# Dummy matmuls ahead of the first scores, two kinds of load on another queue, and 1.5 instead of 1.2 conversion steps a unit, in a fused decay-attention and MLP kernel

## The chip, the core and the metric

The kernel runs on one core of a Trainium2 chip. The metric is device microseconds of one execution; the time of a kernel is the median of its runs. The page of the profile shows one further execution, recorded by the hardware profiler.

## The reference

Attention with a decay, eight batches of eight heads, 576 positions, 64 channels, followed by an MLP with a squared relu on all 4608 tokens:

```python
scores = scale * np.matmul(q, k.transpose(0, 1, 3, 2))
log_f = np.log(np.clip(f, 0.0001, 1.0))
cum = np.cumsum(log_f, axis=-1)
decay = cum[:, :, :, None] - cum[:, :, None, :]
scores = np.where(causal, -1000000000.0, scores + decay)
scores = scores - np.max(scores, axis=-1, keepdims=True)
attn = np.exp(scores)
attn = attn / (np.sum(attn, axis=-1, keepdims=True) + 1e-09)
x = np.matmul(attn, v)            # then (batch, seq, heads * channels)
h = np.maximum(x @ w_in, 0.0)     # 512 -> 2048
out = h * h @ w_out               # 2048 -> 512
```

The MLP's weights arrive as float64 and are read as pairs of 32-bit words.

## The kernel before

**Slots.** The 64 heads (NH) are taken one after the other, and each head is NU = 6 units of scores; a slot is one unit. The loop at the end of the kernel runs over slots n from -12; the first score is in slot 0. In each slot the program emits the unit's score matmuls and its exponential, the product with V of the unit two slots back (LAG), parts of the division by the denominator (`finish`), the events entered for this slot with `at` (loads, maxima), then conversion steps (`cv`) and, from slot 60, halves of MLP steps (`fill`). Each slot has two halves. The program order of TensorE (PE), ACT, DVE and POOL is this order of tracing, kept by `in_order`. SP only issues DMAs and keeps the order too.

**Heads 0 to 13** (`h < NWHOLE`) use fp32 operands. `load_whole` brings q and k of a head into one of two buffers (`rl` in the profile, L251), two heads ahead, and `load_rounded` brings the same q and k rounded to fp32r through POOL's queue (`rk`, L244). `load_cum` (L236 and L238) adds the rows of the cumulated decay. In the head before, `max_units` computes the row maxima from the rounded copy: six matmuls (L302), each with a reduction on DVE (`tcol`, L308) in two PSUM banks, and five small stores of a column of maxima into a row of the whole q (L314, from SP). A score matmul (L335, masked blocks L337) has q, k, the decay and that row as its 67 rows, so it waits for the store. The exponential is L351 on ACT, the product with V L398, `v` is loaded at L258. `finish` moves denominators through DRAM (L423, L428, L431) and multiplies at L434.

**Weights.** `weight_ops` is a generator. `stage` loads one of 32 blocks of 512 KB (L164), up to four blocks ahead of the conversion; five steps convert a block from float64 words to a pair of fp32r parts: four operations on DVE (L184, L189, L194, L196), an absolute value and a copy on ACT (L173, L201), a subtraction on POOL (L202). `convert(n)` takes n steps. RATES gives the steps a slot: slots before -6, slots -6 to -1, slots 0 to 47, and later ones.

**MLP.** Token chunks of 256: `mlp1` has 12 matmuls (L464) and `mlp2` 6 (L487) for each of 16 blocks of the hidden layer. They start at slot 60, on the block pairs that are converted by then, are paced over the remaining slots of a batch, and go on alone after the last head.

**PSUM.** Bank 7 is unused until the first MLP chunk takes it as `o1`. `mz` is a bf16 tile of 128x448, zero but for its last 128 columns (a causal mask).

**Semaphores.** In the compiled program the DMAs of SP carry eight semaphores in turn, and an issue waits until the eighth DMA before it has landed.

Of the kernel before, what the change touches and what calls it, by code (L numbers as in the profile page):

```python
# [9 lines left out]
F32 = mybir.dt.float32  # L10
F32R = mybir.dt.float32r
I32 = mybir.dt.int32
# [21 lines left out]
def decay_attention_relu2_kernel(  # L34
# [18 lines left out]
    nc = tc.nc  # L53

    NH, D, _, S = qk.shape
    P = 2 * D
# [21 lines left out]
    psum = ctx.enter_context(tc.tile_pool(name="psum", bufs=1, space=bass.MemoryType.PSUM))  # L78
# [3 lines left out]
    def bank(use):  # L82
# [7 lines left out]
    MW = 448  # L90
    mz = cpool.tile([P, MW], BF16, name="mz")
    nc.gpsimd.memset(mz, 0.0)
    nc.gpsimd.affine_select(
        out=mz[:, MW - P:], in_=mz[:, MW - P:], pattern=[[-1, P]],
# [6 lines left out]
        out=eye, in_=eye, pattern=[[-1, P]],  # L101
# [23 lines left out]
    def load_f():  # L125
        nc.sync.dma_start(out=fr[:NH, 0, :], in_=f)
# [29 lines left out]
    def weight_ops():  # L156

        staged, mags = {}, {}

        def stage():  # L160
            i = len(staged)
            if i < NW:
                raw = staged[i] = wk.tile([P, 2 * DM], I32, name=f"w{i}", bufs=1)
                nc.sync.dma_start(out=raw, in_=(w_in, w_out)[i % 2][i // 2].bitcast(I32))  # L164

        def words(i):
            w = staged[i].rearrange("p (n t) -> p n t", t=2)
            return w[:, :, 0], w[:, :, 1]

        def magnitude(i):  # L170
            if i < NW:
                mags[i] = wk.tile([P, DM], F32, name="wmag", bufs=1)
                nc.scalar.activation(out=mags[i], in_=words(i)[1].bitcast(F32), func=AF.Abs)  # L173

        stage()
        stage()
        yield
        magnitude(0)
        yield
        for i in range(NW):  # L180
            low, high = words(i)
            mag = mags.pop(i)

            nc.vector.tensor_scalar(mag, mag, MAG_LOW, MAG_HIGH, ALU.max, ALU.min)  # L184
            yield
            w = wk.tile([P, DM], F32, name="osb")
            wi = w.bitcast(I32)

            nc.vector.tensor_scalar(  # L189
                wi, mag.bitcast(I32), 3, 0x3FFFFFFF, ALU.logical_shift_left, ALU.bitwise_and,  # L190
            )
            magnitude(i + 1)
            yield
            nc.vector.scalar_tensor_tensor(wi, high, -0x40000000, wi, ALU.bitwise_and, ALU.bitwise_or)  # L194
            yield
            nc.vector.scalar_tensor_tensor(wi, low, 29, wi, ALU.logical_shift_right, ALU.bitwise_or)  # L196
            while len(staged) < min(i + 1 + DEPTH, NW):
                stage()
            yield
            hl = wk.tile([P, 2, DM], F32R, name=f"w{i}", bufs=1)  # L200
            nc.scalar.copy(out=hl[:, 0], in_=w)  # L201
            nc.gpsimd.tensor_tensor(out=hl[:, 1], in0=w, in1=hl[:, 0].bitcast(F32), op=ALU.subtract)  # L202
            split_w.append(hl)
            yield
# [17 lines left out]
    NU = len(UNITS)  # L222
# [9 lines left out]
    def load_cum(h, k):  # L232

        if h == 0:
            for i, c in enumerate(cum):
                nc.sync.dma_start(out=f32(k[D + i:D + i + 1, :]), in_=c[h:h + 1])  # L236
        else:
            nc.sync.dma_start(out=f32(k[D:D + 2, :]), in_=cum_dr[h])  # L238

    def load_rounded(h):  # L240

        x = rounded[h % 2]
        state[h] = dict(r2=x[:, 0], kl0=x[:, 1], p={})
        nc.gpsimd.dma_start(out=x[:D], in_=qk[h])  # L244
        if cum:
            load_cum(h, x[:, 1])

    def load_whole(h):

        x = state[h]["whole"] = whole[h % 2]  # L250
        nc.sync.dma_start(out=x[:D], in_=qk[h])  # L251
        if cum:
            load_cum(h, x[:, 1])

# [278 lines left out]

    RATES = (1, 2, 1.2, 2.5)
    LAG = 2
    NA = H * NU

# [2 lines left out]
    MAXIMA = (0, 0.5, 1, 1.5, 2, 2.5), (1.5, 2, 2.5, 3, 3.5, 4)  # L542
# [48 lines left out]
    def cv(k):  # L591
        owed[0] += k
        convert(int(owed[0]))
        owed[0] -= int(owed[0])
# [3 lines left out]
    def at(n, half, do, *args):  # L598
        events.setdefault((n, half), []).append(lambda: do(*args))
# [6 lines left out]
    for h in range(NH):  # L606
        split = h >= NWHOLE
        if split:
            at((h - 2) * NU + LOAD, 0, load, h)
            for part in range(4):  # L610
                at((h - 1) * NU + SPLIT[part], 1, prep, h, part)
        else:
            if h > 1:
                at((h - 3) * NU + 3, 0, load_rounded, h)
                at((h - 2) * NU + 5, 1, load_whole, h)
        at((h - 1) * NU + VLOAD, 1, load_v, h)
        at((h - 1) * NU + VSPLIT, 1, split_v, h)
        for i, x in enumerate(MAXIMA[split]):
            at((h - 1) * NU + int(x), int(2 * x) % 2, max_unit, h, i)
    for b in range(B):  # L620
        at(ready[b] - 2, 0, split_x, b * S // T, b + 1)
    load_f()
    load_rounded(0)
    convert(1)
    load_whole(0)
    decay()
    load_cum(0, rounded[0][:, 1])
    load_cum(0, whole[0][:, 1])
    store_cum()
    load_rounded(1)  # L630
    load_whole(1)
    for n in range(-2 * NU, last_slot + 1):
        live = 0 <= n < len(slots)
        split_last()
        if live:
            h, u = slots[n]
# [11 lines left out]
        for do in events.get((n, 0), ()):  # L648
            do()
        wr = RATES[0 if n < -NU else 1 if n < 0 else 2 if n < NA else 3]  # L650
        cv(wr / 2)
# [49 lines left out]
```

## Time and profile before

| | us |
|---|---|
| median of three runs | 1267.6 |
| the three runs | 1256.87, 1269.65, 1267.6 |
| span of the profiled execution, its own time on the page | 1272.5 |
| PE busy | 1225.8 |
| DVE busy | 780.7 |
| ACT busy | 703.2 |
| POOL busy | 368.3 |

The profiled execution is 2.9 us above the slowest of the three runs; the page gives no time outside its span. A row of the timeline has start, duration, engine, line, operation, output<-input, shape, count, and in brackets how long the engine sat idle before it and what ended that. A row of the table of windows has, for a stretch of the span, the busy time of each engine with its instructions, the granted TensorE clock (1.00 is full), the share of the DMA engines and the GB/s. SPq is SP's queue of DMA issues.

### The profile page before, as it was taken

The numbers are of one execution on the slowest core, as the hardware profiler recorded it, in microseconds if no ns is written. First come the engines' busy times: TensorE is split into PE (matmuls) and PEld (weight loads), VectorE is DVE, ScalarE is ACT, GpSimd is POOL, SyncE is SP. The second block draws the span as 40 slices with busy tenths as digits, with TensorE's granted clock in tenths as the row PEclk, the third lists the DMA queues.
The fourth block names the chain that finished last, engine by engine and source line by source line (L and its number), as shares of the span: only waits on it lengthen the run. The fifth ranks groups of instructions, "written<-read, shape, count | busy, mean of one in ns | idle before, by whom it ended". The sixth has DMA issues, their size and how long they took to land.

```text
span 1272.5 us, 23177 instructions
## 1 busy us (share of the span) xinstructions
PE 1225.8 (96%) x7652; PEld 1064.1 (84%) x7652; DVE 780.7 (61%) x2042; ACT 703.2 (55%) x1720; POOL 368.3 (29%) x508
## 2 busy tenths in 40 slices
PE   3997899999999999999999999999999999999998
PEld 2664578788999889999899989998998989999997
DVE  6354887666676667665665576667666767533322
ACT  3453455456666666665656566666666666632332
POOL 3122323333333433332232233333333433200000
PEclk9997699999999999999999999999999999999999
DMA  8566661102121112111111111212121211100000
GB/s 198 117 148 140 158 165 31 52 20 56 40 57 40 52 40 56 38 43 46 33 37 44 35 38 40 57 40 56 40 57 38 53 40 47 26 27 1 17 18 17
DMA packets 115639, 71.90 MB, mean 57 GB/s; under 512 B 97384, under 2 KB 97384, under 8 KB 115520
## 3 DMA queue, kind: packets, MB, share of 16 engines
q1 hardware_dynamic: 114400, 66.30, 21.5%
q0 software_dynamic: 1120, 4.13, 1.5%
q8 instruction: 61, 1.00, 0.3%
q14 instruction: 58, 0.48, 0.1%
HBM read 60.20 MB, written 9.88 MB: 55 GB/s over the span
## 4 chain that ended last, share of the span: by engine, by line
PE 63%; ACT 2%; issue 1%; POOL 1%; DVE 0%; DMA 0%; SPq 0%; POOLq 0%; DVEq 0%
PE bank L464 25%; PE bank L487 24%; PE bank L377 3%; PE bank L344 2%; PE bank L379 2%; PE bank L378 2%; PE bank L302 2%; PE bank L341 2%; ACT ph L366 0%; ACT den L413 0%; ACT r L472 0%; DMA den<-rdr 0%; ACT p L351 0%; POOL v L289 0%; POOL p L353 0%
## 5 line engine op out<-in xcount | busy, mean ns | idle before, releaser
L487 PE MATMUL bank<-w,gh 128*128 128x512 f32 x1152 | 413.6, 400 | 0.0
L464 PE MATMUL bank<-xh,w 128*128 128x256 f32 x2304 | 331.1, 286 | 2.9 <-DVE tcol L308 2.9
L367 DVE TENSOR_TENSOR pl<-p,ph 128x320 fp32r<-128x320 f32 (+4 forms) x300 | 186.2, 621 | 210.3 <-ACT ph L366 200.8
L464 PEld LDWEIGHTS bank<-xh,w 128*128 128x128 f32 x2304 | 301.7, 190 | 12.4 <-DVE tcol L308 3.5
L487 PEld LDWEIGHTS bank<-w,gh 128*128 128x128 f32 x1152 | 217.4, 189 | 39.0
L487 PE MATMUL bank<-w,gl 128*128 128x512 f32 x576 | 226.9, 394 | 0.2 <-DVE gl L475 0.2
L472 ACT ACTIVATE r<-bank 128x256 f32<-128x256 f32 x288 | 110.6, 384 | 209.2 <-PE bank L464 196.6
L473 DVE TENSOR_TENSOR g<-r 128x256 f32<-128x256 f32 x288 | 129.0, 448 | 143.5 <-ACT r L472 142.8
L353 POOL TENSOR_SCALAR_AFFINE_SELECT p<-p 128x128 f32<-128x128 f32 (+1 forms) x250 | 81.0, 324 | 450.5 <-ACT p L351 292.8
L366 ACT CAST ph<-p 128x320 fp32r<-128x320 f32 (+4 forms) x300 | 124.4, 415 | 149.0 <-POOL p L353 147.3
L464 PE MATMUL bank<-xl,w 128*128 128x256 f32 x1152 | 185.3, 283 | 0.0
L308 DVE CUSTOM_DVE_ANT_0 bank<-bank,mz 128x256 f32<-128x256 f32 (+4 forms) x320 | 133.8, 432 | 68.4 <-PE bank L302 67.1
L464 PEld LDWEIGHTS bank<-xl,w 128*128 128x128 f32 x1152 | 158.8, 191 | 0.0
L351 ACT ACTIVATE p<-bank 128x320 f32<-128x320 f32 (+4 forms) x300 | 116.0, 387 | 70.6 <-PE bank L344 66.6
L475 DVE TENSOR_TENSOR gl<-g,gh 128x256 fp32r<-128x256 f32 x288 | 126.3, 438 | 35.4 <-DVE g L473 0.9
L302 PE MATMUL bank<-rk 66*128 66x320 f32 (+4 forms) x384 | 119.0, 340 | 21.5 <-DMA rk<-qkraw 14.3
L474 ACT ACTIVATE gh<-r 128x256 fp32r<-128x256 f32 x288 | 120.5, 418 | 9.1
L487 PEld LDWEIGHTS bank<-w,gl 128*128 128x128 f32 x576 | 109.2, 190 | 14.3 <-DVE gl L475 0.9
L302 PEld LDWEIGHTS bank<-rk 66*128 66x128 f32 (+1 forms) x384 | 73.3, 198 | 40.3 <-issue 18.6
L377 PE MATMUL bank<-pl,vh 128*65 128x320 f32 (+4 forms) x350 | 99.4, 284 | 1.7 <-ACT den L413 1.5
L378 PE MATMUL bank<-ph,v 128*64 128x320 f32 (+4 forms) x350 | 94.8, 271 | 0.0
L379 PE MATMUL bank<-ph,vh 128*65 128x320 f32 (+4 forms) x350 | 93.0, 272 | 0.0
(66 smaller groups left out, 1531.6 us busy)
## 6 DMA issues: line engine op xcount, KB each, us to landing
qkraw<-in_qk SPq DMA_DIRECT2D x50, 288.0 KB
v<-in_v SPq DMA_DIRECT2D x64, 160.0 KB
den<-rdr SPq DMA_DIRECT2D x64, 144.0 KB
out<-osb SPq DMA_DIRECT2D x36, 256.0 KB
w<-in_w_in SPq DMA_DIRECT2D x16, 512.0 KB
w<-in_w_out SPq DMA_DIRECT2D x16, 512.0 KB
rl<-in_qk SPq DMA_DIRECT2D x14, 288.0 KB
rk<-in_qk POOLq DMA_DIRECT2D x14, 288.0 KB, 5.2
```

The lines of the kernel that those rows point to most:

```text
L302: nc.tensor.matmul(ps[:m, :n], st["r2"][:D + 2, q0:q0 + m], st["kl0"][:D + 2, k0:k0 + n], start=True, stop=True,)
L308: nc.vector.tensor_tensor_reduce(out=ps[:m, :n], in0=ps[:m, :n], in1=mz[:m, mo:mo + n], op0=ALU.add, op1=ALU.min, scale=-1.0, scalar=init, ...
L366: nc.scalar.copy(out=ph[:kn, :n], in_=p[:kn, :n])
L367: nc.vector.tensor_tensor(out=pl[:kn, :n], in0=p[:kn, :n], in1=ph[:kn, :n].bitcast(F32), op=ALU.subtract,)
L377: nc.tensor.matmul(acc[:D + 1, o], vh, pl[:kn, i], start=first, stop=False)
L378: nc.tensor.matmul(acc[:D, o], vl, ph[:kn, i], start=False, stop=False)
L379: nc.tensor.matmul(acc[:D + 1, o], vh, ph[:kn, i], start=False, stop=last)
L464: nc.tensor.matmul(ph[:, :T], w[:, s, cc], x[:, cc, :], start=(cc == 0 and k == 0), stop=(cc == NCC - 1 and k == 2),)
L473: nc.vector.tensor_tensor(out=g, in0=r, in1=r, op=ALU.mult)
L474: nc.scalar.activation(out=gh, in_=r, func=AF.Square)
L475: nc.vector.tensor_tensor(out=gl, in0=g, in1=gh.bitcast(F32), op=ALU.subtract)
L487: nc.tensor.matmul(po, g[:, ts], w[:, s], start=(fc == 0 and k == 0), stop=(fc == NF - 1 and k == 2),)
```

## The change

Four edits. (1) 24 matmuls are put at the very start of PE's program; two more follow each of head 0's first five maxima and 14 the last one: 48 in all. Each is `mz[:, :128]` (zeros) times `mz`, bf16, 128x128 by 128x448, into bank 7, whose content is used by nobody. (2) The weight blocks are loaded from ACT's queue. (3) The whole q and k of heads 2 to 13 are loaded from ACT's queue; heads 0 and 1 stay on SP's. (4) In slots 0 to 47 a slot has 1.5 conversion steps and not 1.2.

```diff
-                nc.sync.dma_start(out=raw, in_=(w_in, w_out)[i % 2][i // 2].bitcast(I32))
+                nc.scalar.dma_start(out=raw, in_=(w_in, w_out)[i % 2][i // 2].bitcast(I32))
...
-        nc.sync.dma_start(out=x[:D], in_=qk[h])
+        (nc.scalar if h > 1 else nc.sync).dma_start(out=x[:D], in_=qk[h])
...
-    RATES = (1, 2, 1.2, 2.5)
+    RATES = (1, 2, 1.5, 2.5)
...
+    spun = psum.tile([P, 512], F32, name="bank7")
+
+    def spin(n):
+
+        for _ in range(n):
+            nc.tensor.matmul(spun[:, :MW], mz[:, :P], mz, start=True, stop=True)
+
+    for i in range(5):
+        at(int(MAXIMA[False][i]) - NU, int(2 * MAXIMA[False][i]) % 2, spin, 2)
+    at(int(MAXIMA[False][5]) - NU, int(2 * MAXIMA[False][5]) % 2, spin, 14)
+    spin(24)
     load_f()
     load_rounded(0)
     convert(1)
```

## The prediction

> **What bounds the kernel now.** First the slices of the span on the page.
>
> ```profile
> PE   3997899999999999999999999999999999999998
> ...
> PEclk9997699999999999999999999999999999999999
> DMA  8566661102121112111111111212121211100000
> ```
>
> PE is busy nearly all the time, so a microsecond that PE gains early arrives at the end unless a later wait takes it back. Only the first seven slices have holes, and two have a reduced clock; the change works there. Next, windows cut at the heads' first score matmuls: heads 1 to 3, 5, 7, 9, 10 and 11.
>
> ```profile
> 34.39:47.88 13.49, 13.49 (x38) 8.18 (x37) 5.00 (x17) 5.45 (x14) 2.56 (x4) 1.00 0.55 130
> 47.88:61.38 13.50, 13.50 (x39) 8.18 (x38) 6.75 (x20) 5.75 (x14) 2.63 (x4) 1.00 0.42 103
> 61.38:74.87 13.49, 13.49 (x38) 8.18 (x38) 6.69 (x17) 5.00 (x13) 3.28 (x4) 1.00 0.68 154
> ...
> 86.68:98.41 11.73, 7.79 (x40) 4.82 (x38) 6.31 (x18) 6.49 (x15) 2.90 (x4) 1.00 0.93 192
> ...
> 108.90:122.73 13.83, 7.47 (x39) 4.76 (x38) 6.92 (x18) 5.83 (x15) 4.60 (x5) 0.86 0.84 183
> ...
> 134.49:148.42 13.93, 12.08 (x39) 6.63 (x37) 12.00 (x28) 7.83 (x17) 6.60 (x7) 0.68 1.02 235
> 148.42:174.20 25.78, 22.88 (x117) 18.02 (x116) 19.06 (x39) 10.19 (x24) 5.49 (x6) 0.78 0.57 136
> 174.20:195.16 20.96, 20.12 (x118) 16.06 (x117) 16.59 (x36) 11.69 (x28) 5.45 (x5) 1.00 0.61 176
> ```
>
> Heads 1 to 3 take 13.5 us each, with PE busy throughout and a clock shown as 1.00. That 1.00 is not to be believed: here is one form of score matmul in head 2 and in head 5, from the timeline of PE.
>
> ```profile
> 50.66 1.27 PE L335 MATMUL bank<-rl 67*128 67x320 f32 x2
> 51.72 0.31 PE L337 MATMUL bank<-p,mz 128*128 128x128 bf16 x1
> ...
> 88.14 0.70 PE L335 MATMUL bank<-rl 67*128 67x320 f32 x2
> ```
>
> The same work takes 1.27 and 0.70 us. So until about 84.8 us PE ran at half clock, and the view has no record of it. With the clock up, PE is done with head 5 after some 7.8 us (its busy time in the window from 86.68) and then idles. Windows cut where durations change show the clock after that; under them, PE's waits between 14 and 240 us.
>
> ```profile
> 84.78:98.43 13.65, 9.71 (x49) 5.89 (x47) 6.74 (x19) 7.12 (x16) 4.46 (x5) 1.00 0.94 192
> ...
> 118.91:132.56 13.65, 9.83 (x28) 6.38 (x29) 6.60 (x18) 4.67 (x10) 2.29 (x2) 0.50 0.44 88
> ...
> 139.39:159.87 20.48, 17.08 (x50) 10.79 (x51) 14.97 (x30) 8.25 (x19) 7.07 (x7) 0.50 0.71 169
> ...
> PE bank L302 <- DMA rk<-qkraw: 14.3, 1, 14.3
> PE bank L335 <- issue: 5.7, 1, 5.7
> ...
> PE bank L335 <- DMA rl<-tcol: 3.8, 1, 3.8
> ```
>
> At full clock PE outruns the loads, waits 3.8 or 5.7 us at the end of heads 5 and 7 for a store of maxima, and the clock halves; then the slow head hides the next stores, and the clock rises again. All edges lie multiples of 3.41 us apart: 4 of them from 84.78 to 98.43, 6 from 98.43 to 118.91, and so on. What raises the clock I estimate from the matmuls of one stretch:
>
> ```profile
> 23.34:159.87 136.53, 121.48 (x391) 75.32 (x392) 77.64 (x209) 60.04 (x138) 36.72 (x43) 0.85 0.62 140
> ```
>
> For each 3.41 us piece of it I added every matmul's streaming time, weighted by its active rows over 128: 66 or 67 for maxima and scores, 128 for L337, L398 and L464. Streaming times are scaled from the gapless fp32 score of 320 columns, 1.06 us at half clock (50.66 to 51.72), and a quarter of that per column for fp32r and bf16. The clock rose after pieces with a share of 0.756 to 0.77, never after 0.755 or less; it fell after 0.35 or less and stayed after 0.466 or more. Attention alone gives 0.5 to 0.77, so whether it rises depends on how the pieces happen to fall on a head.
>
> **The change part by part.** *Dummy matmuls.* The nearest row in streaming is the MLP's first group at half clock, 12 matmuls of 256 columns in 2.73 us (up to the next L302); `mz` is ready at 1.65.
>
> ```profile
> 1.36 0.29 POOL L93 TENSOR_SCALAR_AFFINE_SELECT mz<-mz 128x128 bf16<-128x128 bf16 x1
> ...
> 14.31 0.82 PE L302 MATMUL bank<-rk 66*128 66x256 f32 x2 [14.31 <-DMA rk<-qkraw]
> ...
> 18.26 0.31 PE L302 MATMUL bank<-rk 66*64 66x64 f32 x1 [0.48 <-DVE tcol L308]
> ...
> 23.16 1.41 PE L335 MATMUL bank<-rl 67*128 67x320 f32 x2 [4.59 <-DMA w<-in_w_out]
> ...
> 154.04 2.08 PE L464 MATMUL bank<-xh,w 128*128 128x256 f32 x8 [2.90 <-DVE tcol L308]
> ...
> 156.77 0.47 PE L302 MATMUL bank<-rk 66*128 66x320 f32 x1
> ```
>
> That is 0.23 us for 256 columns, so 0.40 for 448, and 0.20 at full clock. The first 24 take 4.8 to 9.6 us, end by 11.3 and lie beside the wait to 14.31; a clock that they raise is lost again in the rest of that wait. The other 24 use all 128 rows, with few gaps from the first maximum on, a share near 1: a piece that begins after 14.3 raises the clock by about 21 us, before the first score. Their price: ten of them, 4.0 us at half clock, stand between maxima that DVE spaces anyway (3.95 us from first to last), and 14 need 2.8 to 5.6 us in a wait of 4.6. The first score is late by between 0 and 2 us; I take +1. No row shows that zeros count like data; that is a rival.
>
> [...]
>
> *Heads 0 to 3*, 51.71 us (23.16 to 74.87), would then run as heads 4 to 7 do, 47.86 us (74.87 to 122.73) or 11.97 each, with the clock going up and down. *Moved loads.* The queues at the end of head 5:
>
> ```profile
> 90.33 0.58 SPq L164 DMA_DIRECT2D w<-in_w_in  x1
> ...
> 91.00 1.12 SPq L431 DMA_DIRECT2D den<-rdr  x2
> ...
> 92.21 1.83 SPq L314 DMA_DIRECT2D rl<-tcol  x3
> ...
> 92.33 0.56 POOL L244 DMA_DIRECT2D rk<-in_qk  x1
> ...
> 94.13 0.60 SPq L258 DMA_DIRECT2D v<-in_v  x1
> ...
> 94.83 0.90 SPq L314 DMA_DIRECT2D rl<-tcol  x1
> ...
> 98.38 0.48 PEld L335 LDWEIGHTS bank<-rl 67*128 67x128 f32 x2 [3.90 <-DMA rl<-tcol]
> ```
>
> SP loses 1.44 weight issues a head (7.2 steps, five a block) and one of `rl`, 2.44 by 0.58 = 1.4 us, of which I count half as standing ahead of the stores: -0.7 a head. The same bytes still come. With the DMA engines at 0.94 the last store needs 2.6 us from the end of its issue to the score, and POOL's load, on a queue of its own, shares those engines, so another queue need not let a store overtake. Bounds: 0 to -3.8 a head, the whole wait. *Rate 1.5* adds 0.36 block, 0.19 MB, a head; at head 9's 235 GB/s that is 0.8 us where DMA decides and nothing where it does not: +0.2. So 11.5 a head: -5.8 for heads 0 to 3, -2.0 for heads 4 to 7.
>
> On ACT the 32 + 12 issues cost what they cost SP: 2.8 a head by 0.58, 1.6 us. ACT was busy 5.4 us in heads 1 to 3 (mean), at most 6.8 if all of it grew with the rate: 8.4 of 11.5. Behind a waiting issue stand exponentials, and PE's product with V waits for those; two units of lag cover them. I cost this at 0; without the cover it is rival C.
>
> *Start.* Three weight loads no longer stand ahead of the two rows of cumulated decay in SP's queue:
>
> ```profile
> 0.81 0.58 SPq L126 DMA_DIRECT2D xt<-in_f  x1
> ...
> 3.59 0.64 DVE L132 TENSOR_SCALAR xt<-xt 64x576 f32<-64x576 f32 x1 [0.76 <-DMA xt<-in_f]
> ...
> 6.85 1.31 SPq L236 DMA_DIRECT2D rk<-qkraw  x2
> ```
>
> These issues end at 8.16; f, alone on the engines, was used 2.2 after its issue, so 10.4 instead of 14.3 is the best: 0 to -3.9, and I take half, -2. *Heads 8 and 9* keep their 2.5 steps and their DMA load (1.02 in head 9): -1, of 0 to -4. *Head 10* took 25.78 against 20.96 for the next, with the clock down until 159.87: half the difference, -2.4. *Conversion* ends at slot 76 instead of 82 (91.0 instead of 76.6 of 162 steps are done by slot 48); there PE has three short waits for DVE, 3.3 us in all up to 320 us: -1, of 0 to -3.
>
> ```profile
> PE bank L302 <- DVE tcol L308: 3.3, 3, 1.4
> ```
>
> Sum: +1 -5.8 -2.0 -2 -1 -2.4 -1 = -13.2, on the profiled execution's own 1272.5: 1259.3. That execution lies 4.9 above the median. How long the first stretch stays at half clock depends on where the pieces fall, so I take half of the -5.8 as a gain that the median has already: -10.3 from 1267.6, **1257**.
>
> **Rivals.** *A, the clock holds.* For it: a share of 0.466 is enough to keep the clock. Then a head costs PE 7.9 us and DMA 8.2 (the mean of heads 1 to 3, 1.74 MB, plus 0.19, at 235 GB/s); with 1 us of waiting for a store, 9.2. Heads 0 to 7 go from 99.6 to 73.6, -26; with -1 at the start, -4, -4.8 and -1: -36.8, and with the 2.9 given back, 1234. Against it: both heads that ended at full clock without MLP work beside them waited 3.8 and 5.7. *B, it does not do what it says*: zeros don't raise the clock, or the next pieces lose it at once, and stores stay behind loads. The 14 dummies cost 1.5, and +1.5 -2 -2 -1 -1 gives 1263. The rows from 92.33 to 98.38 speak for its second half. [...] *C, slower.* ACT's in-order queue carries 44 issues, 25.5 us at SP's price, and each waits for the eighth DMA before it, as SP once did for 2.0 us:
>
> ```profile
> SPq L164 <- DMA w<-in_w_out: 2.0, 1, 2.0
> ```
>
> I estimate 1 us for every fourth weight block, 8. If all of it reaches PE: 1257 + 33.5 = 1290. It decides once ACT's waits pass 3.1 us a head (11.5 less 8.4). Against it: the waits are rare on SP, and ACT has that slack.
>
> **How the numbers follow.** Chances: the forecast 0.54, A 0.15, B 0.24, C 0.07. The forecast's own bounds, from the terms above, reach some 12 us down and 8 up; B lies inside. The range takes those in, reaches a little into A's side, and leaves out most of A and all of C: 1242 to 1269. One per cent, about what can be told from no change in this kernel, is 1254.9 to 1280.3. Faster takes A, nearly half of the forecast and a little of B: 0.42; slower is C, 0.07; the rest is 0.51.
>
> **What would show it.** Right: scores of 320 columns at 0.70 us in head 0; heads of 10 to 12 us with gaps at their ends, and half clock after the gaps; first maxima before 14 us; no L164 in SP's queue. Wrong: 1.27 us still in heads 1 to 3 (B); heads near 9 us without gaps (A); exponentials that start late behind ACT's DMA issues while DVE and DMA have time (C).

## The result and the profile after

The change makes the kernel a little slower. The median is 1271.5 us (20 runs, 1261.9 to 1280.4) against 1263.3 us for the kernel before (20 runs, 1256.8 to 1275.6); the ratio is 1.0065, with a 95% interval of 1.0037 to 1.0094. The forecast was 1257, with a range of 1242 to 1269. The profiled execution took 1266.0 us (span 1264.3), 5.5 below its own median; the profile of before, with a span of 1272.5, lay some 11 us above a typical span of its kernel (1263.3 less the 1.7 us that lie around the span here). Read side by side, these two profiles therefore show a gain that the medians don't have.

First the slices of the span and the two hardware queues of the changed kernel's page (packets, MB, share of the DMA engines).

```profile
PE   5987899999999999999999999999999999999998
PEclk8777699999999999999999999999999999999999
...
q1 hardware_dynamic: 108832, 45.98, 15.8%
q10 hardware_dynamic: 5568, 20.32, 5.5%
```

The move was made: 20.32 MB, 32 weight blocks and 12 heads' q and k, now go through ACT's queue (q10). The holes in PE's first slices and the reduced clock beside them are no fewer than before. The start, in the timeline of the changed kernel (SP's issues, one ACT issue, one DVE operation, PE):

```profile
0.81 0.57 SPq L126 DMA_DIRECT2D xt<-in_f  x1
1.44 0.57 SPq L251 DMA_DIRECT2D rl<-in_qk  x1
2.06 2.58 SPq L258 DMA_DIRECT2D v<-in_v  x3
9.27 1.33 SPq L236 DMA_DIRECT2D rk<-qkraw  x2
...
20.70 0.50 SPq L229 DMA_DIRECT2D qkraw<-in_qk  x1
21.29 1.84 SPq L314 DMA_DIRECT2D rl<-tcol  x3
...
0.82 0.38 ACTq L164 DMA_DIRECT2D w<-in_w_in  x1
...
6.20 0.45 DVE L132 TENSOR_SCALAR xt<-xt 64x576 f32<-64x576 f32 x1 [3.37 <-DMA xt<-in_f]
...
17.34 0.55 PE L302 MATMUL bank<-rk 66*128 66x256 f32 x1 [8.92 <-DMA rk<-qkraw]
...
22.69 2.92 PE L627 MATMUL bank<-mz 128*128 128x448 bf16 x14
28.91 0.78 PE L335 MATMUL bank<-rl 67*128 67x320 f32 x2 [3.30 <-DMA rl<-tcol]
29.84 1.27 PE L335 MATMUL bank<-rl 67*128 67x320 f32 x2
```

f was used at 3.59 us before and is used at 6.20 now: a weight block goes out at the same moment on the other queue, and three loads of v follow f on SP's own (e4 below splits the two). The rows of cumulated decay are computed from f, and their issue starts at 9.27 instead of 6.85. The decay is also stored, in two parts, which are out of SP's queue by 10.70 in before. Now the second part goes out at 14.17, as its issue waits until a load of v has landed, the DMA that had carried its semaphore before (SP's waits up to 26 us: us in total, times, longest):

```profile
SPq L146 <- DMA v<-in_v: 1.1, 1, 1.1
```

The load of the stored decay follows at 19.94 instead of 15.04, and behind it the stores of maxima begin at 21.29 instead of 16.69. The first maxima come at 17.34 instead of 14.31, and the first score at 28.91 instead of 23.16. This corrects a sentence of the part on the kernel: SP does not keep the order of the code. `in_order` names only PE, ACT, DVE and POOL; SP's issues are placed by the framework's scheduler, which filled SP's freed time with v and with q and k of head 14 (20.70).

Windows of the changed kernel (start:end and length, busy time of PE, its weight loads, DVE, ACT, POOL, then granted clock, DMA share, GB/s): the last zeros, the wait behind them, the stretch after the clock was lost, heads 0 to 3, 4 to 7, 8 and 9, 10, and the rest.

```profile
22.90:25.60 2.70, 2.70 (x14) 1.18 (x12) 2.56 (x6) 0.99 (x2) 1.80 (x3) 1.00 0.68 150
25.60:28.91 3.31, 0.01 (x1) 0.03 (x1) 1.59 (x4) 0.58 (x2) 0.00 (x0) 1.00 0.39 98
...
29.73:46.80 17.07, 17.07 (x50) 10.67 (x48) 9.85 (x30) 7.50 (x17) 3.80 (x6) 0.50 0.49 133
...
28.91:70.80 41.89, 39.32 (x142) 24.72 (x142) 26.57 (x79) 21.17 (x50) 11.37 (x16) 0.71 0.61 154
70.80:118.75 47.95, 36.91 (x151) 22.15 (x149) 31.38 (x82) 23.88 (x57) 16.08 (x19) 0.82 0.72 168
118.75:144.12 25.37, 23.39 (x74) 14.14 (x74) 20.18 (x45) 13.26 (x29) 10.16 (x11) 0.63 0.65 177
144.12:170.56 26.44, 22.69 (x117) 17.87 (x117) 20.22 (x43) 11.52 (x27) 6.60 (x6) 0.77 0.42 109
170.56:1264.30 1093.74, 1084.38 (x7169) 973.95 (x7167) 667.16 (x1762) 626.19 (x1549) 315.93 (x436) 1.00 0.17 40
```

The same stretches of before (head 10 took 25.78):

```profile
23.16:74.87 51.71, 51.71 (x142) 31.45 (x143) 25.66 (x73) 20.43 (x48) 11.54 (x15) 1.00 0.61 135
74.87:122.73 47.86, 37.56 (x150) 23.87 (x149) 24.19 (x76) 22.38 (x53) 13.07 (x16) 0.89 0.64 139
122.73:148.42 25.69, 23.84 (x74) 14.06 (x74) 20.46 (x47) 13.71 (x30) 9.73 (x11) 0.63 0.67 159
...
174.20:1272.50 1098.30, 1086.75 (x7169) 975.13 (x7167) 676.53 (x1775) 628.78 (x1556) 319.25 (x439) 1.00 0.17 42
```

The zeros did raise the clock (1.00 from 22.90), but PE then idles 3.31 us for the stores of maxima and the clock halves at 29.73, 0.82 us after the first score. What the zeros were to buy is gone before it is used. Between the two profiles: +5.7 to the first score, -9.8 in heads 0 to 3, +0.1, -0.3 and +0.7 in the next groups, -4.6 from head 11 on.

### The profile page after: what moved, and what is told of

Same layout as the page of the kernel before. It is cut to its first block, busy times and chain, and to the rows that moved or that the text cites. A ratio compares the mean times of both kernels' runs of the same rounds, so it can differ in the third digit from the quotient of the medians.

```text
span 1264.3 us, 23245 instructions
## 1 busy us (share of the span) xinstructions
PE 1221.7 (97%) x7700; PEld 1059.9 (84%) x7700; DVE 781.3 (62%) x2042; ACT 703.8 (56%) x1720; POOL 369.2 (29%) x508
## 3 DMA queue, kind: packets, MB, share of 16 engines
q10 hardware_dynamic: 5568, 20.32, 5.5%
## 5 line engine op out<-in xcount | busy, mean ns | idle before, releaser
L475 DVE TENSOR_TENSOR gl<-g,gh 128x256 fp32r<-128x256 f32 x288 | 129.2, 449 | 35.8 <-DVE g L473 0.5
```

The costliest lines, as they stand in the source:

```text
L475: nc.vector.tensor_tensor(out=gl, in0=g, in1=gh.bitcast(F32), op=ALU.subtract)
```

## The experiments

All ratios are to the kernel before, run beside it on the same chip; a ratio is not the quotient of the two medians and differs from it by up to 0.3%. The theory at the outset: the moved loads cost by a later start, and the zeros' clock is lost in the next wait. The rivals: ACT's queue costs in every head, or the zeros or the rate cost.

**The three parts alone**

```
e1: + the 48 matmuls of zeros            e3: RATES = (1, 2, 1.5, 2.5)
e2: stage(): nc.scalar.dma_start(...)    load_whole: (nc.scalar if h > 1 else nc.sync).dma_start(...)
e4: the whole change, and in_order(..., ("PE", "Activation", "DVE", "Pool", "SP"))
```

> The kernel before with the 48 dummy matmuls alone. Theory H (SP's reordered start made the change slower): the dummies are harmless or help; SP's order is that of before, the first score is at 23 to 24.5 us, scores of 320 columns run at 0.70 us in head 0, and the time is 0 to 6 us under before. Theory S (ACT's issues) says the same of this run. Theory D (the dummies themselves cost): 3 to 8 us over before, with a late first score.

> The kernel before with the two kinds of load on ACT's queue alone. Theory H: SP's scheduler, no longer held by the weight blocks, issues three loads of v ahead of the cumulated rows, and the load of q and k of head 14 ahead of the first stores of maxima; first maxima at 17 us, first score at 27 to 29 us, and the time 4 to 10 us over before. Theory S (ACT's in-order issues delay exponentials): also slower by 4 to 10 us, but spread over heads 0 to 9, each 0.5 to 1 us longer, with the first score not later than 25. Theory D: within 2 us of before.

> The kernel before with 1.5 conversion steps a unit alone. Theory H: within 3 us of before, first score at 23.2. Theory R (the extra weight blocks compete for the DMA engines in the first heads): 3 to 8 us over before, heads 4 to 9 longer by 0.5 to 1 us each.

> The changed kernel whole, with SP's issues held in the order of tracing as the other engines' are. Theory H: first maxima at 12 to 14 us, first score at 19 to 24, and the time 5 to 12 us under the changed kernel, so 0 to 5 under before. Theory S: the first score moves, but the time stays within 3 us of the changed kernel's, 6 to 9 over before. Theory R: likewise 3 to 8 over before.

Measured: zeros 1269.2 us, ratio 1.0033 (0.9999 to 1.0066); moved loads 1275.4, 1.0097 (1.0058 to 1.0135); rate 1261.6, 0.9987 (0.9952 to 1.0023); SP in the order of the code 1273.0, 1.0079 (1.0046 to 1.0111). The moved loads are the cost, the rate is nothing that can be told, the zeros gain nothing: their time is the one that theory D named, without the late first score that it went with. PE's timeline with the zeros alone, and the windows up to the clock's fall and from there to its next rise:

```profile
22.29 0.78 PE L335 MATMUL bank<-rl 67*128 67x320 f32 x2
...
23.18 0.70 PE L335 MATMUL bank<-rl 67*128 67x320 f32 x2
...
22.29:25.90 3.61, 2.84 (x12) 1.72 (x12) 3.33 (x10) 2.01 (x5) 1.31 (x2) 1.00 0.99 237
25.90:43.00 17.10, 16.98 (x49) 10.33 (x48) 9.38 (x29) 6.71 (x16) 3.87 (x5) 0.50 0.50 121
```

Here the zeros do all that was hoped: the first score is not late and runs at 0.70 us. The clock is lost 3.61 us later all the same, in attention that kept PE busy for 2.84 of them, and rises again at 43.0. SP in the order of the code did bring the first maxima forward, yet not the time (DVE's first use of f, SP's wait, then PE):

```profile
5.24 0.54 DVE L132 TENSOR_SCALAR xt<-xt 64x576 f32<-64x576 f32 x1 [2.41 <-DMA xt<-in_f]
...
17.75 0.32 SPq L238 DMA_DIRECT2D rk<-cum_dr  x1
...
11.34 0.36 PE L302 MATMUL bank<-rk 66*128 66x256 f32 x1 [2.31 <-DMA rk<-qkraw]
25.45 1.41 PE L335 MATMUL bank<-rl 67*128 67x320 f32 x2 [6.82 <-DMA rl<-tcol]
```

SP now stands until 17.75 for the stored decay, and the stores of the maxima computed from 11.34 on stand behind it. Here no v goes ahead, and f is used at 5.24: of the 2.6 us by which it is late in the whole change, 1.65 come without the loads of v and 1.0 with them.

**The start, one queue each, and before again**

```
e5: the whole change, but stage(): (nc.scalar if i > 5 else nc.sync).dma_start(...)
e6: the kernel before, stage() alone on nc.scalar
e7: SP's first 20 issues in a written order, all but two weight blocks after the first maxima's stores; RATES = (0, 2, 1.5, 2.5)
e8: the kernel before, unchanged
e9: the kernel before, load_whole alone on nc.scalar for h > 1
```

> The whole change, but with the first six weight blocks left on SP's queue, so that SP issues its first loads in the order of before. Theory S (the cost of the moved loads is the later start: f shares the engines with weights, SP issues v first, first score 28.91 instead of 23.16): f lands before 4.0 us, first maxima at 14 to 15, first score 22 to 24, and the time falls from 1271.5 to about 1264 (ratio to before 0.997 to 1.003). Rival T (the cost lies in the later heads, by stores that wait beside loads of another queue or by ACT's issues): first score early, but 1269 or more (ratio 1.004 and up).

> The kernel before with the weight blocks alone on ACT's queue; the q and k loads stay on SP. Theory S: f lands near 6 us and the first score comes at 28 to 29 as with both moves, time 1270 to 1276 (ratio 1.005 to 1.010). Rival U (the q and k loads on ACT, which wait there behind exponentials, are the costly part): first score may be late, but the time is within 3 us of before (ratio under 1.003).

> The kernel before with SP's first twenty issues in an order written out: f, one weight block, the rows of cumulated decay, their store, the second block, head 1's rows, the first maxima's stores, and only then the other blocks; no conversion steps before slot -9, 1.5 a unit later. Theory S (the order of the first loads decides): first maxima at 10 to 12 us, first score at 17 to 20, time 1258 to 1261 (ratio 0.994 to 0.998). Rival V (an early start is given back, since the weight blocks then arrive later and the first heads wait for stores and v, as when all of SP's order was pinned): first score before 21, but head 4 starts no earlier than 70 us at a like clock, and the time is 1263 or more.

> The kernel before once more, for a second profile. Theory W (the half clock up to 84.8 us was one execution's luck): the clock is up before 60 us, heads 0 to 3 take at most 47 us together instead of 51.7, and the span is 1268 or less. Rival X (the kernel before always sleeps that long): scores of 320 columns at 1.27 us up to head 3 or 4, heads 0 to 3 in 50 us or more, span 1270 to 1275.

> The kernel before with only the q and k loads of heads 2 to 13 on ACT's queue; SP's first issues stand as in before. Theory S (the moved loads cost by the start alone): first score at 22 to 25 us, time within 2 us of before (ratio 0.998 to 1.002). Rival T (later heads lose too, since SP's order changes there and stores wait): first score as before, but ratio 1.003 or more.

With the start kept: first score at 23.19, 1269.1 us, ratio 1.0010 (0.9973 to 1.0047), where the whole change has 1.0065. The medians say less: 4.8 us above the kernel before (1264.3), where the whole change was 8.2 above its own. The 12 runs lie in two groups, five from 1257 to 1262 and seven from 1269 to 1274. So theory S has the ratio on its side, rival T the time. Weights alone on ACT: 1271.5, 1.0048 (1.0011 to 1.0085), with the late start of the whole change, as theory S had it. PE in these two:

```profile
23.19 0.78 PE L335 MATMUL bank<-rl 67*128 67x320 f32 x2 [0.55 <-DMA rl<-tcol]
```

```profile
17.51 0.82 PE L302 MATMUL bank<-rk 66*128 66x256 f32 x2 [17.51 <-DMA rk<-qkraw]
29.04 1.40 PE L335 MATMUL bank<-rl 67*128 67x320 f32 x2 [6.40 <-DMA rl<-tcol]
```

The second copy of before explains the largest term of the forecast. Its PE, and its windows of heads 0 to 3 and from head 11 on:

```profile
38.38 1.27 PE L335 MATMUL bank<-rl 67*128 67x320 f32 x2
...
47.84 0.70 PE L335 MATMUL bank<-rl 67*128 67x320 f32 x2
...
24.38:67.17 42.79, 39.90 (x142) 25.41 (x142) 24.16 (x73) 20.31 (x48) 11.58 (x15) 0.92 0.70 151
...
166.91:1265.70 1098.79, 1086.31 (x7169) 975.21 (x7167) 676.09 (x1775) 628.72 (x1556) 320.12 (x439) 1.00 0.17 41
```

The same program woke at 43.1 us instead of 84.8, and its heads 0 to 3 took 42.79 us, against 51.71 in the first profile and 41.89 with the change. So the half clock up to 84.8 was an unlucky draw (theory W). How rare it is, two profiles can't tell, but in e9, e15, e17 and e18 below, with 67-row scores and no zeros either, the clock first rises at 41.0 to 42.1 (in e7, e6, e2 and e13 at 57.6 to 82.1). The record of the clock begins with its first rise, so an execution that is long although its recorded clock is high has likely lost the time before: of 147 executions of the kernel before beside the experiments, 15 took 1268 us or more at a recorded clock of 0.98 or more on average, as the first profile did (0.983).

The early start was a miss: first maxima at 11.37, first score at 18.16, yet 1265.3 us, ratio 1.0026 (0.9991 to 1.0060). Head 0 then takes 16.07 us instead of 11.23, and head 4 starts at 70.59: rival V. And q and k alone on ACT, with the first score at 22.84 as in before, are slower: 1270.9, 1.0038 (1.0010 to 1.0067). So rival T holds beside S: the start is not the whole cost. PE's waits in that kernel name stores of maxima (us in total, times, longest):

```profile
PE bank L335 <- DMA rl<-tcol: 16.2, 5, 4.5
```

The copy of before has fewer of them, with the clock up for nearly as long between 40 and 155 us (50.4 us against 51.9, by the clock records):

```profile
PE bank L335 <- DMA rl<-tcol: 4.6, 2, 2.3
```

The first of these rows includes 4.0 us ahead of the first score, which in the copy stand under another name (4.3 us). Behind the first score and under all names, scores wait 15.3 us in e9 and 6.1 in the copy.

**Rows, not zeros**

The prediction's estimate of what raises the clock weighted PE's time by active rows. If that holds, the cure is not zeros ahead of the scores but all 128 rows in the scores: rows 67 to 127 of the whole q and k are zeroed once, and a score takes no longer (1.27 us at half clock with 67 rows, in the copy of before, and with 128, in e10).

```
e10:  r, k = st["whole"][:, 0], st["whole"][:, 1]     # was [:D + 3]
      for x in whole: nc.gpsimd.memset(x[D:], 0.0); constants in rows D to D + 2
e11:  e10 + the 48 zeros + rate 1.5          e12:  e10 + rate 1.5
e14:  e7 + e10                               e16:  the whole change + e10
```

> The kernel before, with the fp32 scores of heads 0 to 13 taken over all 128 rows (rows 67 to 127 hold zeros) instead of 67; columns, passes and everything else as before. Theory R (what raises and keeps the clock is PE's streaming time weighted by active rows, so attention alone stays near the threshold and 48 zeros can only lend it two stretches): scores of 320 columns at 0.70 us within 10 us of the first score, half clock only after waits, heads 0 to 7 in 75 to 90 us instead of 99.6, time 1245 to 1257 (ratio 0.985 to 0.995). Rival P (rows don't count; the moment of waking is luck): the same spread of waking times as before and a ratio of 0.998 to 1.002.

> The same 128-row scores, with the change's 48 matmuls of zeros and its 1.5 conversion steps, all loads on SP's queue as in before. Theory R: the zeros raise the clock before the first score and the scores now keep it, so it is 1 to 4 us faster than the 128-row scores alone: 1243 to 1254. Rival Z (the zeros only cost, clock or not): 0 to 4 us slower than the 128-row scores alone.

> The kernel before with 128-row scores and 1.5 conversion steps a unit; no zeros, no moved loads. If the zeros are worth nothing once the clock holds by itself, this equals the run with both, 1251 to 1255 (ratio 0.990 to 0.993); if they still raise the clock ahead of the first score to some use, it is 2 us or more slower than with them, 1255 or more; if they only cost, it is 2 us or more faster, 1251 or less.

> 128-row scores with the first twenty of SP's issues in the written order and no conversion before the first maxima, 1.5 steps a unit later. Theory S (the start counts when the clock holds): first score at 17 to 20 us and 3 to 6 us less than with the rows alone: 1247 to 1251 (ratio 0.986 to 0.990). Rival V (what the start gains, later loads take back): head 4 starts no earlier than with the rows alone (61.3 us) and 1252 or more.

> The whole change, with 128-row scores added. If the moved loads cost by their late start whatever the clock does, first score at 28 to 29 us and 4 to 8 us more than with rows, zeros and rate (1253.0): 1257 to 1261, ratio 0.994 to 0.998. If with the clock up the later start is hidden: 1255 or less.

128-row scores alone: 1253.4 us, ratio 0.9910 (0.9878 to 0.9943), faster than both kernels. PE's timeline and the windows of heads 0 to 3, 4 to 7 and from head 11 on:

```profile
25.33 1.27 PE L335 MATMUL bank<-rl 128*128 128x320 f32 x2
...
29.09 0.33 PE L335 MATMUL bank<-rl 128*64 128x64 f32 x2
...
33.51 0.70 PE L335 MATMUL bank<-rl 128*128 128x320 f32 x2
...
23.64:61.34 37.70, 30.71 (x142) 19.96 (x142) 24.47 (x74) 20.82 (x49) 12.33 (x16) 1.00 0.89 179
61.34:105.37 44.03, 33.35 (x148) 21.07 (x149) 25.07 (x76) 21.80 (x51) 12.67 (x16) 0.92 0.69 156
...
155.49:1253.00 1097.51, 1086.03 (x7169) 975.52 (x7167) 680.59 (x1775) 627.96 (x1556) 318.64 (x439) 1.00 0.17 41
```

A score takes 1.27 us at half clock, as with 67 rows, but the clock is up by 29.1, 5.5 us after the first score. Heads 0 to 7 take 81.7 us, against 99.6 and 92.5 (24.38 to 116.86) in the two profiles of before. Rows count; theory R of this run holds. With zeros and rate added: 1253.0, 0.9922 (0.9896 to 0.9949); with the rate alone: 1252.5, 0.9926 (0.9896 to 0.9957). The zeros are worth nothing that can be told even then. The rate gives back what it brings, by the windows of e12:

```profile
22.35:63.11 40.76, 30.36 (x142) 19.34 (x143) 29.33 (x80) 22.32 (x52) 12.97 (x17) 0.96 0.85 177
63.11:109.44 46.33, 33.49 (x149) 21.01 (x149) 29.60 (x81) 22.97 (x54) 14.98 (x18) 0.87 0.67 159
...
160.26:1253.50 1093.24, 1084.58 (x7169) 973.92 (x7167) 663.06 (x1762) 625.78 (x1549) 314.92 (x436) 1.00 0.17 40
```

From head 11 on it is 4.3 us shorter, and heads 0 to 7 are 5.4 us longer, with DVE busy 59 us instead of 50; these are one profile each, and that of e12 is among the slowest of its 12 runs. The early start with 128-row scores was given back again: 1259.5, 0.9981 (0.9953 to 1.0009), head 0 taking 13.64 us after a first score at 19.29; it even lies 6 to 7 us above the two kernels with 128-row scores and the late start, and no run says why. And the whole change with 128-row scores takes 1262.0, 0.9999 (0.9969 to 1.0029): the moved loads cost 9 us against e11 with the clock up too, with the first score at 29.23 against 21.86.

**Why q and k cost on ACT's queue**

```
e13:  q and k on nc.scalar, issued at((h - 1) * NU + 3, 0, ...)     # was at((h - 2) * NU + 5, 1, ...)
e15:  the same at((h - 1) * NU, 1, ...)
e17:  the kernel before with "SP" added to in_order                  e18:  e17 + e9
```

> The kernel before with the q and k loads of heads 2 to 13 on ACT's queue, but issued three units into the head before, behind that head's stores of maxima instead of ahead of them. If the moved loads cost because they start at once beside the stores (theory E, early sharing), the stores land within 2.9 us of their issue as in before and the ratio is 0.996 to 1.002; if the queue or ACT's issue itself costs (theory Q), the ratio stays at 1.003 or more.

> The q and k loads of heads 2 to 13 on ACT's queue, issued one unit after the moment of before (half a unit into the next head). Theory E (on ACT they go out too early and share the engines with the stores): ratio 0.997 to 1.002, PE's waits for stores of maxima up to 240 us below 12 us. Theory Q (the queue costs, whatever the moment): 1.003 to 1.006. Theory L (on this path every unit later costs, as three units did): 1.006 or more, with PE waiting for q and k.

> The kernel before with SP's issues in the order of the code. The third weight block then stands behind the rows of cumulated decay: first maxima at 11.5 to 13.5 us instead of 14.3, first score at 20 to 23, ratio 0.996 to 1.002.

> The same with the q and k loads of heads 2 to 13 on ACT's queue, SP's other issues in the same order. Theory O (the order that the scheduler chose was the cost): within 2 us of the same kernel without the move. Theory Q (the second queue itself): 4 to 7 us slower than it.

Three and a half units later was too late and tells nothing of the queue: 1290.6 us, 1.0232 (1.0186 to 1.0279). PE then waits for q and k themselves:

```profile
PE bank L340 <- DMA rl<-in_qk: 9.0, 2, 5.2
```

One unit later: 1267.8, 1.0049 (1.0010 to 1.0087). The cost stayed, which speaks against early sharing (theory E), as far as one later moment can. PE's waits settle nothing here: scores wait 12.8 us behind the first, against 15.3 in e9, but the clock is up for 40.9 us between 40 and 155, against 51.9.

SP in the order of the code costs the kernel before 1.0098 by itself (1275.4 us; 1.0057 to 1.0139): a miss, since its first maxima are early as expected (12.87) but SP then waits for the stored decay, and the first score comes at 24.85. With q and k moved, the same order gives 1277.7, 1.0122 (1.0074 to 1.0169). The 0.24% between the two lies inside the intervals, and their 2.3 us lie between what theory O (the order which the scheduler chooses for SP's other issues is the cost) and theory Q (the second queue itself) named. It also takes the verdict from e4: the fixed order that was to mend the start costs about as much as it could have brought.

The traces say more than the times. Against theory O: but for the loads of q and k themselves, SP's first 143 issues in e9, up to 148 us, stand in the order of before except in three places, by the names of what they load and store. For theory Q: what changes is how long SP stands ahead of the stores of maxima until some DMA has landed. From 24 to 165 us, in e9, the copy of before and e15 (L319 is L314 there):

```profile
SPq L314 <- DMA rl<-in_qk: 9.7, 3, 4.9
```

```profile
SPq L314 <- DMA rl<-tcol: 0.3, 1, 0.3
```

```profile
SPq L319 <- DMA rl<-in_qk: 3.8, 2, 2.0
```

In these traces SP's and ACT's DMAs carry the same eight semaphores (in the changed kernel 715 issues of SP and 44 of ACT), so a store on SP can have to wait for a load on ACT. In e9 the load of 91.37 and the next store share one; the load lands at 96.34, and the store goes out at 96.40, 3.0 us after its maximum was ready (0.8 in the copy). From the moment at which a head's last maximum is ready to the issue of its last store, it takes 23.8 us over heads 1 to 10 in e9, against 16.6 and 17.4 in the two profiles of before: 6 to 7 us more, about the cost. But it is 19.8 in e15, whose cost is as large, and 23.9 in e18 against 21.2 in e17. So this is likely a part of the cost; how much, no run tells, since none gives ACT's queue semaphores of its own.

## Why the prediction was wrong, step by step

The forecast took 10.6 us off a base of 1267.6, the median of three runs; the median of 20 is 1263.3. So the change itself was missed by 18.8 us: -10.6 forecast, +8.2 measured.

**The start, -2, measured +5.7 (+4.5 from the copy of before): the step that failed first.** It took weights out of SP's queue and left the rest in place. But the order of that queue was not fixed, and the queue itself had been a priority: f was issued 0.63 us ahead of the first weight block. On two queues a block goes out with f, v right behind it, and f is used 2.6 us later; then a store of the decay waits for the landing of v, and the stores of maxima begin 4.6 us late. Keeping the first six blocks on SP brings the first score back to 23.19 and the ratio from 1.0065 to 1.0010; those intervals just overlap, and the medians moved by less (8.2 to 4.8 us). A queue of its own for the block did not leave f alone: in e4, where no v goes ahead, f is still used at 5.24 instead of 3.59.

**Heads 0 to 3, -5.8, of which half was counted.** A second execution of the kernel before had nearly all of it already: 42.79 us against 41.89 with the change. The prediction saw that the wake depends on how pieces fall, and then took one execution for half of the typical. Its border between pieces that raise the clock and others, 0.756 against 0.755, also comes from that one execution; that rows count is shown, a border so sharp is not.

**The zeros.** Right: zeros raise the clock, at 22.9 us (about 21 forecast), and 14 of them cost 2.92 us at full clock (2.8). Wrong: that heads 0 to 3 then run like heads 4 to 7. Rival B's "the next pieces lose it at once" is what happened, in the wait of 3.31 us here and, with the zeros alone, 3.6 us into the first head.

**Heads 4 to 10.** -2.0, -1 and -2.4 were forecast; the two profiles give +0.1, -0.3 and +0.7, and against the copy of before -1.7, +2.8 and -1.0. "Another queue need not let a store overtake" was right. That the moved q and k loads would only help was not: they cost 0.38% with the start unchanged. By which way stays open: SP's order hardly changes, while the semaphores that the two queues share delay SP's stores, which is likely a part of it but was not tested alone.

**Conversion, -1.** From head 11 on the profiles show -4.6, but by the profile of e12 heads 0 to 7 pay it back; measured alone, the rate gives -0.13% (-0.48 to +0.23).

**Rival C** had the sign right and the mechanism wrong. ACT does stand at its issues, once for 5.9 us ahead of the load of 118.73 in the changed kernel, but PE was waiting for a store of maxima then, and in that profile no wait of PE up to 240 us names ACT. The 1290 us that it named came only where q and k were late.

The sum of the parts measured alone, +0.33, +0.97 and -0.13%, is 1.2%; the whole is 0.65%. With intervals of about 0.35% on each, these agree. The profiles don't show where all of it goes: from the copy of before to the changed kernel they give -1.4 us, one lying some 4 us above its kernel's median and the other 5.5 below.

## What to carry to other kernels

A load moved to a second queue loses its place behind the urgent ones (here f was used at 6.20 us instead of 3.59), and the freed queue may be filled by something else (here by three loads of v): look up the order that the scheduler gives it, and whose landings its issues wait for, before a gain is counted. Where the moment at which the clock rises varies from run to run (84.8 and 43.1 us in two profiles of the kernel before), one profile is one draw; take a second one of the kernel before, then change what raised the clock here (rows in the matmuls themselves, ratio 0.9910) rather than adding work ahead of them (ratio 1.0033).

## What the runs showed of the hardware

Rows count for the clock. The same scores, as long as before (1.27 us at half clock), taken over 128 rows instead of 67, raised it within 5.5 us of the first one in e10 and made the kernel 0.9% faster. In the two other profiles with 128 rows and no zeros it rose 3.3 us after the first score (e12) and, across a wait in head 0, 11.4 us after it (e14); with 67 rows and no zeros it took from 16 us (e17) to 62 (before). That PE was busy without a gap did not raise it: in the first profile of before, attention, whose scores and maxima use 67 and 66 rows, kept PE busy for all of the 62 us from 23.2 to 84.8 and stayed at half clock.

In the first profile of before the clock's edges lie whole multiples of 3.41 us apart, and the shortest stretch between two of them, from 299.82 to 303.23, is one such piece. Counted in these pieces, the edges are not tied to the program: whole pieces taken off, they lie at 2.86 us in that profile and at 2.14 in its copy. Much of the spread may come from that; no run shows it. A gapless head at half clock takes 13.49 us, 3.95 pieces, so pieces creep by 0.16 us a head. By the clock records, the piece that ended with the clock's first rise behind the first score began 6.5 us after a head's start in before (head 4), and 6.4 to 6.6 after one in e1 (head 1), e7 (head 2) and e2 (head 3); in before the clock did not yet rise after the piece that began 6.34 us after the start of head 3. In the other profiles with 67-row scores it began 3.6 to 4.2 us after one (the copy of before among them) or 1.1 to 1.5. This fits that the number of heads depends on where the first piece fell, but no run sets that. The 20 runs of the changed kernel go from 1261.9 us at a mean granted clock of 0.973 to 1280.4 us at 0.949.
